# A transformer block with its backward pass on one core: w_o in 8 KB rows, P rebuilt between w_o tiles, gradient sections ahead of the last LayerNorm, w_down loads behind w_gate stores

**Chip, cores, metric.** One Trainium2 chip, one core. The metric is device time in microseconds (us), as a median over executions. In the views PE is the matmul engine, DVE the vector engine, ACT the scalar engine, POOL GpSimd and SP the sync engine. A load or store is split over sixteen DMA engines; what GpSimd issues (most stores, the w_up and w_gate loads) goes through queue 0, what the sync engine issues through queue 1.

## The reference

A decode step with adaptive LayerNorm, attention over the last 4096 positions of a key/value cache, and a gated feed-forward block (FFN), and then the gradients of all inputs:

```python
x = A_x                                            # 1 x 1 x 1024
mod = (silu(c) @ w_mod).reshape(1, 6, 1, -1)       # w_mod 1024 x 6144
sa, ca, ga, sb, cb, gb = (mod[:, i] for i in range(6))
h = layernorm(x) * (1 + ca) + sa
x = x + ga * attention(h, k_cache, v_cache, wq, wo)   # 32 heads of 128, 4 kv heads; wo 4096 x 1024
h = layernorm(x) * (1 + cb) + sb
x = x + gb * ((sigmoid(h @ w_gate) * (h @ w_up)) @ w_down)   # 1024 x 3584, 3584 x 1024
out, vjp = jax.vjp(...)                            # and the gradients of everything
# ... cut
```

Only one row of x exists. So a weight is read once (w_q and a part of w_mod a second time, for the gradients) and every weight gradient, an outer product of a column and a row, is written once. The cache gradients are full size (4 x 65536 x 128, twice) and zero outside the last 4096 positions; those zeros are 126 of the 256 MB moved. The kernel writes them in 120 stores of 1 MB and uses them as filler: lists of small integers (`Z_...`) say after which step how many go into GpSimd's DMA queue.

## The kernel before

One large on-chip arena is reused by stage. The parts that matter, with cuts:

```python
# forward: w_o, 2 KB rows
wo_view = A_wo.rearrange("(j p) n -> p j n", p=P)
def load_wo(q4):
    nc.sync.dma_start(out=wo_t[q4], in_=wo_view[:, q4 * 4:(q4 + 1) * 4, :])
# ... cut
# FFN loop, 14 blocks of 256 columns; w_down in 2 buffers, w_up and w_gate in 3
for n in range(NB):
    # ... dug, hh, broadcast of dug, FFN products
    nc.sync.dma_start(out=wd_dram(out_8, n), in_=wd)       # w_down gradient
    if n + 2 < NB:
        load_wd(n + 2)                                     # same buffer: waits for that store
    for j in range(KD):
        ttr(ug[:, :, j, :], ...)                           # DVE: dh2
        outer_act(ug[:, :, j, :], h2[:, j:j + 1], dug_b2)  # ACT: gradient in place
        # ... front(n + 1) at j == 3
    if n + 1 < NB:
        front_dve(n + 1)                                   # DVE: needs w_down of block n + 1
    nc.gpsimd.dma_start(out=dwu_view[...], in_=ug[:, 0, :, :])
    nc.gpsimd.dma_start(out=dwg_view[...], in_=ug[:, 1, :, :])
    zero(Z_FFN[2 * n])
    if n + 3 < NB:
        load_ug(n + 3)                                     # 512 B rows
    zero(Z_FFN[2 * n + 1])
# ... cut: broadcasts, P rebuilt; then dw_o tile by tile, w_q reloaded behind it
# last loop: w_q gradient, key/value gradients (two buffers), sections of the w_mod gradient
for i in range(KD):
    # ... dwq store
    grad_kv(gkv[8 * i:8 * i + 8], Z_DKV[i])                # PE, ACT copies to a buffer, store
    if i % 2 == 1:
        sec(2 + i // 2, Z_SEC[2 + i // 2])                 # DVE, store of 1 MB
# ... LayerNorm tail, dx and x2 through one row buffer, then:
sec(6, Z_SEC[6])
sec(7, Z_SEC[7])
for j in range(KD):
    # ... last eight stores, 512 KB each (ACT and DVE in turn)
    nc.gpsimd.dma_start(out=dwm_view[:, j, 0:2048], in_=s2_t[j])
```

## Time and profile before

| | before |
|---|---|
| time, three runs | 634.1 us (633.64 to 634.2) |
| profiled span | 632.7 us |
| bytes moved | 256.41 MB, 405 GB/s over the span |
| busy PE / DVE / ACT | 30% / 50% / 35% |

The DMA row and the table of stages are shown in the prediction. I read them with one more figure, the loss of a stage: its length less its bytes divided by 427 GB/s, the rate at which zeros alone are stored. It comes from the sizes and times of the trace's packets (the single transfers of the DMA engines). Before, in us: 3.6 in the first 8 us; 1.1 up to 100; 2.2 from there to the FFN; 14.3 in the FFN loop; 1.1 from there to 580; and 9.9 after 580.

### The profile page before, as it was taken

Reading aid. Unit: us, or ns where it says so; the run is one execution under the profiler, and the core shown is the slowest. Engines: PE = TensorE matmul, PEld = TensorE weight load, DVE = VectorE, ACT = ScalarE, POOL = GpSimd, SP = SyncE. Lnnn points to the kernel's source line nnn. Section 1 sums busy time; section 2 is a strip of 40 time slices with the busy share of each in tenths; the row PEclk is TensorE's granted clock in tenths of the full one; section 3 lists DMA queues with packets and bytes.
Section 4 is the critical chain, followed back from the end, with each engine's and each line's share of the span. In section 5 each row is a group of like instructions: output and inputs, shape, how many; then the busy total and the mean of one; then the engine's idle time right before and its main releaser. Section 6 shows DMA issues by size and latency. Waiting matters only on the chain.

```text
span 632.7 us, 8339 instructions
## 1 busy us (share of the span) xinstructions
PE 191.6 (30%) x3288; PEld 168.7 (27%) x3288; DVE 319.5 (50%) x708; ACT 222.5 (35%) x342; POOL 142.3 (22%) x224
## 2 busy tenths in 40 slices
PE   3865626650120211111111111115107800055600
PEld 3865624550120211111111111115105700044500
DVE  2532106500069383867527574467995800998060
ACT  1641215610000160613325333335696700055650
POOL 1100200220322213333135331432222211122120
PEclk9966659755555555555555555555555555555555
DMA  9999999999999999999999999999999999999976
GB/s 334 424 422 422 421 419 420 410 421 407 419 427 424 357 415 405 410 384 401 419 401 389 402 400 417 407 414 412 416 423 422 418 424 425 419 428 424 425 322 262
DMA packets 46279, 256.41 MB, mean 405 GB/s; under 512 B 4768, under 2 KB 4768, under 8 KB 23712
## 3 DMA queue, kind: packets, MB, share of 16 engines
q0 software_dynamic: 32128, 192.95, 79.8%
q1 hardware_dynamic: 14064, 62.93, 29.2%
q8 instruction: 25, 0.41, 0.2%
q14 instruction: 14, 0.11, 0.0%
q10 hardware_dynamic: 48, 0.01, 0.0%
HBM read 70.26 MB, written 185.60 MB: 404 GB/s over the span
## 4 chain that ended last, share of the span: by engine, by line
DMA 80%; issue 8%; PE 4%; POOL 3%; DVE 2%; ACT 1%; POOLq 0%; ACTq 0%; SPq 0%; DVEq 0%
DMA out_dram<-arena 28%; DMA out_dram<-zeros 24%; DMA arena<-in_A_wq_dram 9%; DMA arena<-in_A_v_cache_dram 6%; DMA arena<-in_B_w_gate_dram 5%; DMA arena<-in_A_wo_dram 4%; DMA arena<-in_B_w_down_dram 3%; PE tp_kv L401 1%; DMA rows<-in_c_dram 1%; POOL arena L488 1%; DVE junk L174 1%; PE bc_ps L585 1%; POOL out_dram L139 1%; ACT arena L404 0%; PE tp_pT L444 0%
## 5 line engine op out<-in xcount | busy, mean ns | idle before, releaser
L139 POOL DMA_DIRECT2D out_dram<-zeros x120 | 67.2, 565 | 222.6 <-DVE arena L166 43.7
L205 ACT ACTIVATE arena<-dug_b,h 128x512 bf16<-128x512 bf16 x112 | 71.4, 713 | 13.9 <-DVE dh2acc L174 13.9
L174 DVE CUSTOM_DVE_ANT_0 arena<-arena,dug_b 128x512 bf16<-128x512 bf16 x112 | 69.6, 684 | 0.3
L174 DVE CUSTOM_DVE_ANT_0 arena<-arena 128x1024 bf16<-128x1024 bf16 (+1 forms) x16 | 45.1, 2818 | 33.0 <-DMA arena<-in_w_mod_dram 30.7
L561 PE MATMUL gu_ps<-h_bf,arena 128*128 128x1 bf16 x448 | 15.7, 166 | 117.8 <-issue 86.9
L174 DVE CUSTOM_DVE_ANT_0 junk<-arena,b1k 128x1024 fp8e4<-128x1024 bf16 x28 | 34.2, 1223 | 26.4 <-DMA arena<-in_B_w_down_dram 25.9
L738 PEld LDWEIGHTS <-arena 8*128 8x128 bf16 x256 | 25.8, 131 | 76.1 <-issue 72.5
L561 PEld LDWEIGHTS <-arena 128*128 128x128 bf16 x448 | 14.0, 105 | 119.5 <-issue 87.3
L487 POOL DMA_DIRECT2D arena<-in_B_w_up_dram x14 | 12.9, 921 | 107.5 <-DMA out_dram<-arena 77.0
L174 DVE CUSTOM_DVE_ANT_0 arena<-arena,b1k 128x1024 bf16<-128x1024 bf16 x32 | 36.7, 1218 | 0.0
L742 ACT CAST arena<-ps_kv 128x512 bf16<-128x512 f32 x32 | 16.1, 692 | 50.8 <-DMA out_dram<-arena 50.8
L585 PE MATMUL bc_ps<-ident_bf,dug_bf 128*128 128x128 bf16 x56 | 14.5, 475 | 64.2 <-DVE hh L157 64.2
L563 ACT ACTIVATE sg<-gu_ps 128x2 f32<-128x2 f32 x14 | 2.3, 166 | 89.5 <-PE gu_ps L561 89.5
L205 ACT ACTIVATE arena<-b1k,o_col 128x1024 bf16<-128x1024 bf16 x32 | 33.4, 1148 | 0.0
L738 PE MATMUL ps_kv<-DO_hd,arena 8*128 8x128 bf16 x128 | 15.9, 295 | 50.8 <-ACT arena L742 50.8
L401 PE MATMUL tp_kv<-ident_bf,arena 128*128 128x128 bf16 x256 | 22.8, 257 | 22.8 <-DMA arena<-in_A_k_cache_dram 14.0
L313 PEld LDWEIGHTS <-arena 128*128 128x128 bf16 x320 | 28.7, 133 | 1.9 <-issue 1.9
L166 DVE COPY arena<-tp_kv 128x1024 bf16<-128x1024 bf16 x19 | 13.0, 691 | 30.8 <-PE tp_kv L401 30.8
L401 PEld LDWEIGHTS <-arena 128*128 128x128 bf16 x256 | 19.8, 118 | 25.8 <-DMA arena<-in_A_k_cache_dram 14.8
L157 DVE TENSOR_TENSOR dug<-dhh,sg 128x2 f32<-128x2 f32 x14 | 2.3, 161 | 47.2 <-ACT sg L563 46.7
L585 PEld LDWEIGHTS <-dug_bf 128*128 128x128 bf16 x56 | 7.8, 171 | 65.3 <-DVE hh L157 65.3
L404 ACT COPY arena<-tp_kv 128x1024 bf16<-128x1024 bf16 x13 | 13.2, 1012 | 33.9 <-PE tp_kv L401 33.9
(209 smaller groups left out, 504.2 us busy)
## 6 DMA issues: line engine op xcount, KB each, us to landing
out_dram<-zeros POOLq DMA_DIRECT2D x120, 1024.0 KB, 17.0
out_dram<-arena POOLq DMA_DIRECT2D x32, 1024.0 KB, 19.3
out_dram<-arena POOLq DMA_DIRECT2D x36, 512.0 KB, 12.1
arena<-in_A_wq_dram SPq DMA_DIRECT2D x16, 1024.0 KB, 12.4
arena<-in_w_mod_dram SPq DMA_DIRECT2D x8, 1536.0 KB, 18.5
arena<-in_A_wo_dram SPq DMA_DIRECT2D x8, 1024.0 KB, 43.5
arena<-in_B_w_down_dram SPq DMA_DIRECT2D x14, 512.0 KB, 9.3
arena<-in_B_w_up_dram POOLq DMA_DIRECT2D x14, 512.0 KB, 9.7
```

The lines of the kernel that those rows point to most:

```text
L139: ins = nc.gpsimd.dma_start(out=zleft.pop(0).bitcast(FP32), in_=zeros[:, :])
L166: return nc.vector.tensor_copy(out=out, in_=a)
L174: return nc.vector.tensor_tensor_reduce(out=out, in0=w, in1=b, scale=1.0, scalar=0.0, op0=ALU.mult, op1=ALU.add, accum_out=acc)
L205: return nc.scalar.activation(out=out, in_=b, func=ACT.Copy, scale=col)
L313: nc.tensor.transpose(tp[:, nb * P:(nb + 1) * P], wm_t[j][:, c0:c0 + P], ident_bf[:, :])
L401: nc.tensor.transpose(tp[:, t8 * P:(t8 + 1) * P], src[:, g, t_ * DH:(t_ + 1) * DH], ident_bf[:, :])
L404: last = nc.scalar.copy(out=o, in_=tp[:, :])
L487: nc.gpsimd.dma_start(out=ug_slot[n % 3][:, 0, :, :], in_=wu_view[:, :, n * FB:(n + 1) * FB])
L561: nc.tensor.matmul(gu[:, col + jj:col + jj + 1], lhsT=ug[:, k, j, jj::2], rhs=h2_bf[:, j:j + 1], start=(j == 0), stop=(j == KD - 1))
L585: nc.tensor.matmul(ps4[:, k // 2, :, k % 2], lhsT=r["dug_bf"][:, k:k + 1].broadcast_to([P, P]), rhs=ident_bf[:, :], start=(k == 0), stop=( ...
L738: nc.tensor.matmul(ps[:, t4 * DH:(t4 + 1) * DH], lhsT=rows[32 * g:32 * g + HG, t_ * P:(t_ + 1) * P], rhs=hd[32 * g:32 * g + HG, :], start= ...
L742: nc.scalar.copy(out=o, in_=ps[:, :])
```

## The change

Four intents, and new zero lists. w_o and its gradient move in 8 KB rows, which puts the head dimension in another order; o and do are brought into that order by small matmuls. P and the broadcasts are rebuilt between w_o tiles and not ahead of them. The last two gradient sections move into the last loop and x2 is written early, each with its own row buffer. The loads of w_down wait for the w_gate store of their block.

```diff
-Z_FFN = [2, 0, 2, 3, 2, 1, 2, 3, 3, 0, 2, 0, 3, 0, 2, 0, 2, 4, 2, 0, 3, 5, 0, 0, 1, 7, 0, 0]
+Z_FFN = [3, 0, 3, 1, 4, 0, 3, 1, 4, 0, 3, 0, 3, 0, 4, 2, 3, 2, 3, 1, 3, 6, 0, 3, 1, 7, 3, 1]
 ... the other lists too: 36 zero stores asked for ahead of the FFN loop (51 before), 64 in it (49 before)
-        rowb = pool.tile([8, P], BF16, name=name + "_orow", tag="orow")
+        rowb = pool.tile([8, P], BF16, name=name + "_orow", tag=name + "_orow")
+    def wo_rows(t, q4):
+        return t[q4 * 512:(q4 + 1) * 512, :].rearrange("(p j) n -> p (j n)", j=4)
-        nc.sync.dma_start(out=wo_t[q4], in_=wo_view[:, q4 * 4:(q4 + 1) * 4, :])
+        nc.sync.dma_start(out=wo_t[q4], in_=wo_rows(A_wo, q4))
 ... 16 small matmuls that shuffle o, and the like for do
-        if n + 2 < NB:
-            load_wd(n + 2)
 ...
-        nc.gpsimd.dma_start(out=dwg_view[:, :, n * FB:(n + 1) * FB], in_=ug[:, 1, :, :])
+        st = nc.gpsimd.dma_start(out=dwg_view[:, :, n * FB:(n + 1) * FB], in_=ug[:, 1, :, :])
+        if n + 2 < NB:
+            dep(load_wd(n + 2), st)
 ... x2 and its store, up to right after the FFN
-    bcast(dmod_bf[:, 16:48], 32, dmod_b4, "A")
 ... in the dw_o loop:
+            if jj == 3:
+                outer_dve(w, o_sh[:, h:h + 1], dattn_b)
+            else:
+                outer_act(w, o_sh[:, h:h + 1], dattn_b)
+        nc.gpsimd.dma_start(out=wo_rows(out_5, q4), in_=wo_t[q4])
+        if q4 < 2:
+            bcast(dmod_bf[:, 16 + 16 * q4:32 + 16 * q4], 16, dmod_b4[:, 2048 * q4:2048 * (q4 + 1)], "A")
+        elif q4 < 6:
+            rebuild_P(q4 - 2)
+        elif q4 == 6:
+            build_e()
 ... in the last loop:
-        if i % 2 == 1:
-            sec(2 + i // 2, Z_SEC[2 + i // 2])
+        if 1 <= i <= 6:
+            sec(1 + i, Z_SEC[1 + i])
 ...
-    sec(6, Z_SEC[6])
-    sec(7, Z_SEC[7])
```

More of the change, by code (lines that the diff above doesn't have):

```diff
@@ L39 @@
 Z_INIT = 1
-Z_MOD = [0, 1, 3, 0, 0, 2, 0, 0]
-Z_Q = [1, 0, 0, 0, 3, 0, 3, 0]
-Z_K = [1, 1, 0, 0]
-Z_V = [4, 0, 1, 1]
-Z_SM = 5
+Z_MOD = [1, 0, 0, 0, 0, 0, 0, 0]
+Z_Q = [0, 1, 0, 0, 0, 0, 4, 1]
+Z_K = [4, 0, 0, 1]
+Z_V = [1, 2, 0, 0]
+Z_SM = 3
 Z_O = 0
-Z_WO = [0, 0, 1, 0, 4, 0, 8, 1]
-Z_LN = 5
-Z_UG = [0, 0, 5]
-Z_FFN = [2, 0, 2, 3, 2, 1, 2, 3, 3, 0, 2, 0, 3, 0, 2, 0, 2, 4, 2, 0, 3, 5, 0, 0, 1, 7, 0, 0]
+Z_WO = [0, 0, 0, 0, 2, 0, 9, 0]
+Z_LN = 2
+Z_UG = [2, 0, 2]
+Z_FFN = [3, 0, 3, 1, 4, 0, 3, 1, 4, 0, 3, 0, 3, 0, 4, 2, 3, 2, 3, 1, 3, 6, 0, 3, 1, 7, 3, 1]
 Z_T0 = 1
-Z_DWO = [4, 3, 1, 0, 0, 0, 0, 1]
-Z_SEC = [1, 0, 1, 0, 1, 0, 4, 2]
-Z_DWQ = [3, 0, 1, 1, 0, 0, 0, 4]
-Z_DKV = [0, 0, 0, 0, 1, 4, 0, 5]
+Z_DWO = [3, 4, 0, 0, 1, 2, 0, 0]
+Z_SEC = [1, 1, 3, 0, 1, 1, 4, 1]
+Z_DWQ = [1, 0, 0, 1, 0, 0, 0, 6]
+Z_DKV = [0, 0, 4, 0, 3, 3, 1, 5]
 @with_exitstack
@@ L370 @@
     cp(q_col2[:, HQ:2 * HQ], q_ps[:, 0:HQ])
-    wo_view = A_wo.rearrange("(j p) n -> p j n", p=P)
+    def wo_rows(t, q4):
+        return t[q4 * 512:(q4 + 1) * 512, :].rearrange("(p j) n -> p (j n)", j=4)
     wo_off = [40, 48, 56, 32, 0, 8, 16, 24]
-    wo_t = [ar(A_OFF + o, 8).rearrange("p (j n) -> p j n", j=4) for o in wo_off]
+    wo_t = [ar(A_OFF + o, 8) for o in wo_off]
     def load_wo(q4):
-        nc.sync.dma_start(out=wo_t[q4], in_=wo_view[:, q4 * 4:(q4 + 1) * 4, :])
+        nc.sync.dma_start(out=wo_t[q4], in_=wo_rows(A_wo, q4))
     load_kv(A_v_cache, v_nat)
@@ L468 @@
     cp(o_col, o_ps[:, 0:HQ])
+    o_hl = hilo(o_col, HQ, "o_hl").rearrange("p (q a) k -> p q a k", a=4)
+    sh_ps = new_acc("sh_ps")
+    for a in range(4):
+        for jj in range(4):
+            nc.tensor.matmul(sh_ps[32 * a:32 * a + 32, jj * 16:(jj + 1) * 16], lhsT=ident_bf[:, jj::4],
+                             rhs=o_hl[:, :, a, :], start=True, stop=True, tile_position=(0, 32 * a))
+    o_sh = vt([P, HQ], "o_sh")
+    o_shv = o_sh.rearrange("p (q j) -> p j q", j=4)
+    sh_v = sh_ps.rearrange("p (j q k) -> p j q k", j=4, k=2)
+    cp(o_shv, sh_v[:, :, :, 1])
+    addv(o_shv, o_shv, sh_v[:, :, :, 0])
     o_bf = vt([P, HQ], "o_bf", BF16)
-    cp(o_bf, o_col)
+    cp(o_bf, o_sh)
     wg_view = B_w_gate.rearrange("(j p) n -> p j n", p=P)
@@ L483, in load_wd @@
     def load_wd(n):
-        nc.sync.dma_start(out=wd_slot[n % 2], in_=wd_dram(B_w_down, n))
+        return nc.sync.dma_start(out=wd_slot[n % 2], in_=wd_dram(B_w_down, n))
     def load_ug(n):
@@ L492 @@
         for k in range(KD):
-            mm = nc.tensor.matmul(attn_ps[:, k:k + 1], lhsT=wo_t[h // 4][:, h % 4, k * P:(k + 1) * P],
+            mm = nc.tensor.matmul(attn_ps[:, k:k + 1], lhsT=wo_t[h // 4][:, (h % 4) * D + k * P:(h % 4) * D + (k + 1) * P],
                                   rhs=o_bf[:, h:h + 1], start=(h == 0 and k == 0), stop=(h == HQ - 1),
@@ L631 @@
     zero(Z_T0)
+    x2 = vt([P, KD], "x2")
+    mulv(x2, gb, ffn)
+    addv(x2, x2, x1)
+    col_to_row_out(x2, out_0[0], "x2")
     dcs234 = matvec_T([w234_T[:, nb, :] for nb in range(KD)], hilo(dh2, KD, "dh2_hl"), "dcs234")
@@ L659, in sec, with rebuild_P @@
         zero(nz)
-    bcast(dmod_bf[:, 16:48], 32, dmod_b4, "A")
     sec_load(0)
     sec_load(1)
-    for tb in range(4):
+    def rebuild_P(tb):
         tp = new_tp("tp_P")
@@ L673, with build_e @@
         nc.scalar.copy(out=P_bf[:, tb * 1024:(tb + 1) * 1024], in_=tp[:, :])
-    do_col = vt([P, HQ], "do_col")
+    do_sh = vt([P, HQ], "do_sh")
+    e_sh = ar(F_OFF + 16, 1).rearrange("p (j d) -> p j d", j=4)
+    def build_e():
+        ps = new_ps("e_ps")
+        for jj in range(4):
+            for a in range(4):
+                nc.tensor.matmul(ps[32 * a:32 * a + 32, jj * P:(jj + 1) * P], lhsT=ident_bf[:, jj::4], rhs=ident_bf[:, :],
+                                 start=True, stop=True, tile_position=(0, 32 * a))
+        nc.scalar.copy(out=ar(F_OFF + 16, 1), in_=ps[:, :])
@@ L677 @@
     wq_t = [ar(A_OFF + o, 8) for o in wo_off]
-    dwo_view = out_5.rearrange("(j p) n -> p j n", p=P)
     for q4 in range(8):
-        for hh4 in range(4):
-            h = q4 * 4 + hh4
-            w = wo_t[q4][:, hh4, :]
-            ttr(w, w, dattn_b, do_col[:, h:h + 1])
-            outer_act(w, o_col[:, h:h + 1], dattn_b)
-        nc.gpsimd.dma_start(out=dwo_view[:, q4 * 4:(q4 + 1) * 4, :], in_=wo_t[q4])
-        zero(Z_DWO[q4])
+        for jj in range(4):
+            h = q4 * 4 + jj
+            w = wo_t[q4][:, jj * D:(jj + 1) * D]
+            ttr(w, w, dattn_b, do_sh[:, h:h + 1])
+            if jj == 3:
+                outer_dve(w, o_sh[:, h:h + 1], dattn_b)
+            else:
+                outer_act(w, o_sh[:, h:h + 1], dattn_b)
@@ L687 @@
+        nc.gpsimd.dma_start(out=wo_rows(out_5, q4), in_=wo_t[q4])
+        zero(Z_DWO[q4])
+        if q4 < 2:
[4 more added lines that the diff above has]
+            build_e()
         nc.sync.dma_start(out=wq_t[q4], in_=wq_view[:, q4, :])
     do_col2 = vt([P, 2 * HQ], "do_col2", BF16)
-    cp(do_col2[:, 0:HQ], do_col)
-    cp(do_col2[:, HQ:2 * HQ], do_col)
+    do_blk = ar(F_OFF + 17, 0.25)
@@ new lines @@
+    nc.vector.memset(do_blk, 0.0)
+    for a in range(4):
+        cp(do_blk[32 * a:32 * a + 32, a * HQ:(a + 1) * HQ], do_sh[32 * a:32 * a + 32, :])
+    do_bv = do_blk.rearrange("p (n j) -> p n j", j=4)
+    do_ps = new_acc("do_ps")
+    for jj in range(4):
+        nc.tensor.matmul(do_ps[:, 0:HQ], lhsT=e_sh[:, jj, :], rhs=do_bv[:, :, jj], start=(jj == 0), stop=(jj == 3))
+    do_v = do_ps[:, 0:HQ].rearrange("p (a q) -> p q a", a=4)
+    cp(do_col2[:, 0:HQ].rearrange("p (q a) -> p q a", a=4), do_v)
@@ L693 @@
+    cp(do_col2[:, HQ:2 * HQ].rearrange("p (q a) -> p q a", a=4), do_v)
     prod2 = vt([P, 2 * HQ], "prod2")
@@ L773 @@
     col_to_row_out(dx0, out_1[0], "dx0")
-    x2 = vt([P, KD], "x2")
-    mulv(x2, gb, ffn)
-    addv(x2, x2, x1)
-    col_to_row_out(x2, out_0[0], "x2")
-    sec(6, Z_SEC[6])
-    sec(7, Z_SEC[7])
     for j in range(KD):
```

## The prediction

> **What bounds the kernel now.** I read the page first: the busy shares, then the slices, then the DMA queues. No engine is near its limit (PE 30%, DVE 50%, ACT 35%), but the DMA row is full in all but the last two slices:
>
> ```profile
> DMA  9999999999999999999999999999999999999976
> GB/s 334 424 422 422 421 419 420 410 421 407 419 427 424 357 415 405 410 384 401 419 401 389 402 400 417 407 414 412 416 423 422 418 424 425 419 428 424 425 322 262
> DMA packets 46279, 256.41 MB, mean 405 GB/s; under 512 B 4768, under 2 KB 4768, under 8 KB 23712
> ...
> q0 software_dynamic: 32128, 192.95, 79.8%
> q1 hardware_dynamic: 14064, 62.93, 29.2%
> ```
>
> The two queues' shares add up to 109% of the span. So the time is bytes over rate: the change saves only if it moves bytes faster or fills a stretch in which the engines are idle. That has to be seen stage by stage; the windows view is next (columns after the window: busy of PE, weight loads, DVE, ACT, POOL with counts, granted clock, DMA share, GB/s):
>
> ```profile
> 64.00:72.00 8.00, 5.82 (x178) 5.74 (x176) 1.10 (x3) 2.84 (x3) 0.53 (x1) 0.71 1.03 423
> 152.00:164.00 12.00, 3.04 (x96) 2.79 (x96) 0.00 (x0) 0.00 (x0) 2.10 (x4) 0.50 1.07 404
> 176.00:192.00 16.00, 2.96 (x68) 2.82 (x69) 11.61 (x36) 0.20 (x1) 3.19 (x6) 0.50 1.15 427
> 212.00:220.00 8.00, 1.87 (x36) 1.71 (x37) 0.88 (x6) 0.23 (x2) 2.01 (x4) 0.50 1.04 309
> 224.00:440.00 216.00, 38.70 (x750) 35.73 (x750) 130.05 (x402) 81.80 (x157) 69.96 (x97) 0.50 1.12 405
> 440.00:604.00 164.00, 56.70 (x707) 44.79 (x704) 103.14 (x135) 80.01 (x121) 32.39 (x53) 0.51 1.11 423
> 604.00:612.00 8.00, 0.00 (x0) 0.00 (x0) 4.78 (x7) 5.25 (x3) 0.53 (x1) 0.50 0.59 245
> 612.00:628.00 16.00, 0.38 (x1) 0.08 (x1) 4.29 (x13) 0.00 (x0) 5.11 (x9) 0.50 0.96 375
> 628.00:632.70 4.70, 0.00 (x0) 0.00 (x0) 0.00 (x0) 0.00 (x0) 0.00 (x0) 0.50 0.01 3
> ```
>
> Zeros alone (8 KB rows, 176 to 192) go at 427 GB/s. w_q loads in 8 KB rows (64 to 72) reach 423, w_o loads in 2 KB rows (152 to 164) 404, and w_up and w_gate loads in 512 B rows (212 to 220) only 309, with a DMA share over 1: there the engines are busy, but slow. Only one stretch is idle: 604 to 612, share 0.59. At 427 the whole volume would take 256.41 MB / 427 = 600.5 us. The span is 32.2 us above that.
>
> To split the excess I counted the trace's packets in 4 us bins by queue and size and fitted one rate to each kind, as an estimate: zeros and other 8 KB stores 424; w_up and w_gate loads 328 (14.7 MB, 44.8 us, 10.4 over 427); their stores 384 (3.9 us over); w_o and w_mod loads in 2 KB rows 397; the 4 KB packets of dw_o and of the last stores 415. The first 8 us (249 GB/s) lose 3.3 us, the last 33 us about 10.
>
> The hole at 604 is explained by the timelines of POOL, which issues the stores, and of DVE:
>
> ```profile
> 598.74 0.53 POOL L658 DMA_DIRECT2D out_dram<-arena  x1
> 610.19 0.53 POOL L658 DMA_DIRECT2D out_dram<-arena  x1 [10.91 <-DVE arena L170]
> 612.65 0.53 POOL L658 DMA_DIRECT2D out_dram<-arena  x1 [1.93 <-DVE arena L170]
> 613.17 3.52 POOL L787 DMA_DIRECT2D out_dram<-arena  x6
> ```
>
> ```profile
> 602.87 0.17 DVE L157 TENSOR_TENSOR x<-x,x 128x8 f32<-128x8 f32 x1
> 607.15 0.28 DVE L166 CAST x_orow<-rp_x 8x128 bf16<-8x128 f32 x1 [4.11 <-DMA out_dram<-dx_orow]
> ```
>
> For 10.91 us POOL has nothing to issue. It waits for gradient section 6 of w_mod, and DVE makes that late: it first does the LayerNorm tail, then waits 4.11 us until dx_orow has left the one row buffer that x_orow shares. The last eight stores (L787) sit behind sections 6 and 7 in program order, though ACT had the first of them ready at about 603.4.
>
> **What the Trainium skill says.** "DMA: Bandwidth & Descriptors", § Specifications, gives a fabric ceiling of 435 GB/s for the 16 engines; the trace's best stage, 427, agrees, so no stage has hidden head room. § Why small descriptors are slow (HBM only), gives a fixed overhead for each packet, which weighs more the smaller the piece. The order 427, 404, 309 for 8 KB, 2 KB and 512 B rows agrees in direction. § Queues, rings and completion order (Arbitration) says that each engine round-robins between its queues packet by packet. The trace fits that: in 1 us bins in which queue 0 carried almost nothing but w_up and w_gate loads, the total was 303 GB/s with queue 1 empty, and 376 when queue 1 carried about 134 beside them.
>
> **The change part by part.**
>
> *w_o in 8 KB rows.* The 8.4 MB load goes from 397 to about 420 GB/s: 21.2 - 20.0 = 1.2 us. The dw_o store, also 8.4 MB, goes from 415 to 424: 20.2 - 19.8 = 0.4 us. The price is 16 small matmuls and five DVE instructions (0.07 to 0.3 us each) ahead of the w_o products, and as much again at the end of dw_o: 3 us of chain each time. Ahead of the w_o products it is hidden, since PE waits 27.4 us there for w_o to arrive; at the other end the transfers run on. Sum: -1.6 us.
>
> *P and the broadcasts between w_o tiles.* Before, ACT does eight broadcast copies (4.0 us) and four copies of P, and starts the first outer product at 450.88. DVE had the first reduction done at 438.8. So the first dw_o store comes some 12 us earlier. One outer product in four moves to DVE: 8 x 0.35 us more there (a 128x4096 one takes 1.29), 8 x 1.15 less on ACT. But from 440 to 604 the mean is 423 GB/s: queued zeros already fill that wait. What it frees is a few zeros for elsewhere. 0 us.
>
> *gb sections ahead of the last LayerNorm, x2 early, own row buffers.* This takes the 4.11 us wait, about 5 us of DVE work (two reductions of 1.2 and two products of 1.29) and the program order away from the last eight stores. Those then follow as soon as ACT has them, some 5 us after the last key/value gradient is issued, while 2 to 5 MB (5 to 12 us) should still be queued. Data from 604 to 628: 1.96 + 6.0 = 8.0 MB, of which 4.2 MB at 411 and 3.8 at 424 take 19.2 us in place of 24. A ragged end of about 0.9 us remains. Saved: 3.9 us. The 4.7 us after 628 stay.
>
> *w_down loads wait for w_gate stores, zeros dealt out anew.* Bytes are the same; 15 zeros move from ahead of the FFN loop into it (49 to 64). In the trace w_down loads are issued when the w_down store lands, 3 to 25 us before the w_gate store of that block does. They now start then, near the next w_up and w_gate loads. With all 7.3 MB beside such loads, these would run at an effective 350 instead of 328: 44.8 - 42.0 = 2.8 us. But three or four zeros lie in queue 0 between that store and the next load, so much of w_down will meet zeros instead. I take 0.8 us.
>
> Sum: 1.6 + 3.9 + 0.8 = 6.3 us; 634.1 - 6.3 = 627.8.
>
> **The rivals.**
>
> *The FFN loop becomes a chain.* The w_down buffers are two deep, so two blocks now take: w_down load 9.3 us to landing, 2.5 of reduction, 3.5 to the broadcast, 6.5 for the eight reductions and products, and 12.1 for the store to land, about 34 us. The transfers for two blocks are 2 x (3.15 MB + 4.6 zeros of 1.05) = 16 MB, 39 us at 410. So the added zeros cover the chain by 5 us. For the rival: stores took up to 19 us in places and zeros wait behind late stores in POOL's order. If it wins, the loop loses 3 to 10 us, and the total is 631 to 638.
>
> *The stretch ahead of the FFN starves, having 15 zeros fewer.* Against: loads plus remaining zeros there are 72 MB, 171 us, and I count 6 MB or more queued when the last w_o tiles can be asked for. If it happens, up to 4 us are lost: 632.
>
> *Pairing works fully and stores gain as well.* Then 3.5 us instead of 0.8, and the total is 625.
>
> *The hole only moves:* DVE now has 8.1 us of work in a step with a section, against 7.4 us of data (3 MB). But in the trace it had the sixth of these steps done at 578, 20 us before its data left. If it wins, the 3.9 us are lost again: 632.
>
> **How the range follows.** Only the tail is idle time, and rates are capped at 427, so to be over 2% faster (below 621.4) the FFN traffic would have to gain 7 us and the tail everything: 6%. Slower by over 2% needs a stalled FFN loop: 2%. I give 92% to within 2%. The range, 623 to 632, holds the sum with full pairing on one side and one rival coming true on the other.
>
> **What would show it.** Right: no slice below 0.9 of DMA until the last, POOL's 10.91 us wait gone, w_o alone near 420 GB/s, the FFN stretch longer in time (more zeros in it), its loads still near 330. Wrong: DMA shares under 1 inside the FFN loop or between 100 and 180 us, POOL waiting for ACT there, or w_up and w_gate loads near 380, which would make pairing the main gain.

## The result, and the profile after

The changed kernel took 633.34 us (633.23 to 633.42, four runs), the kernel before 634.15 beside it (633.64 to 635.55, four runs). The ratio is 0.9984, with an interval of 0.9966 to 1.0001. A ratio is the mean time of one kernel's fast runs over that of the other's fast runs of the same rounds, so it is not quite the ratio of the medians. "The same" was right; the predicted 627.8 us and its range of 623 to 632 were not.

The page of the changed kernel, its DMA row, its rate by slice and its packets:

```profile
DMA  9999999999999999999999999999999999999986
GB/s 358 422 420 421 420 420 418 425 425 426 420 377 404 400 409 406 400 406 391 395 405 419 400 400 407 421 416 427 415 424 425 423 423 427 420 427 423 398 332 246
DMA packets 42183, 256.42 MB, mean 406 GB/s; under 512 B 4768, under 2 KB 4768, under 8 KB 17568
```

The packets under 8 KB are fewer (23712 before), so the w_o part did its work. The last two slices still move only 332 and 246 GB/s (322 and 262 before). The losses by stage show no gain in the two stages where the prediction put most of its sum: the FFN loop loses what it lost, and the stretch after 580 us 1.3 us more.

| loss against 427 GB/s, us | 0-8 | 8-100 | 100 to FFN | FFN loop | to 580 | after 580 | span |
|---|---|---|---|---|---|---|---|
| before (FFN 208 to 462) | 3.6 | 1.1 | 2.2 | 14.3 | 1.1 | 9.9 | 632.7 |
| after (FFN 172 to 452) | 2.8 | 1.2 | 0.5 | 14.3 | 0.9 | 11.2 | 631.5 |

w_o alone ran at 420 GB/s (404 before), as predicted; a window of the changed kernel, columns as in the prediction:

```profile
128.00:136.00 8.00, 2.89 (x91) 2.64 (x90) 0.00 (x0) 0.00 (x0) 0.00 (x0) 0.50 1.01 420
```

In the FFN loop a wait has grown. First the waits of the kernel before (engine, tile and line, releaser; then total us, count, longest):

```profile
DVE junk L174 <- DMA arena<-in_B_w_down_dram: 25.9, 7, 9.4
...
POOL out_dram L605 <- ACT arena L205: 13.2, 3, 7.4
```

The same waits in the changed kernel, where the stores of w_up's gradient are at L618:

```profile
DVE junk L174 <- DMA arena<-in_B_w_down_dram: 110.8, 12, 20.3
POOL out_dram L618 <- ACT arena L205: 51.0, 9, 11.8
```

DVE now waits 111 us for w_down, and GpSimd 51 us for the gradients that come after it. The chain that ended last shows it too. In the kernel before:

```profile
DMA 80%; issue 8%; PE 4%; POOL 3%; DVE 2%; ACT 1%; POOLq 0%; ACTq 0%; SPq 0%; DVEq 0%
```

In the changed kernel:

```profile
DMA 64%; DVE 17%; PE 7%; issue 5%; ACT 3%; POOL 2%; ACTq 0%; SPq 0%; DVEq 0%; POOLq 0%
```

In the tail the 10.91 us wait for section 6 is gone, but GpSimd waits elsewhere, four times. Timeline of GpSimd in the changed kernel (start, duration, instruction; in brackets the wait before it), where L792 stores a key/value gradient and L826 the last eight; the rows left out store sections and w_q gradients:

```profile
592.41 0.53 POOL L792 DMA_DIRECT2D out_dram<-arena  x1 [10.73 <-ACT arena L790]
...
600.01 0.53 POOL L792 DMA_DIRECT2D out_dram<-arena  x1 [6.02 <-ACT arena L790]
...
607.56 0.53 POOL L792 DMA_DIRECT2D out_dram<-arena  x1 [5.97 <-ACT arena L790]
613.09 1.56 POOL L826 DMA_DIRECT2D out_dram<-arena  x2 [5.00 <-ACT arena L205]
```

And ACT, which makes those gradients, waits for one of its two buffers to have left:

```profile
588.09 4.03 ACT L790 ACTIVATE arena<-ps_kv 128x512 bf16<-128x512 f32 x8 [10.95 <-DMA out_dram<-arena]
```

The new lists also ask for 147 zero stores in all, and there are 120; the last is issued at 561 us (584 before). So I had two first theories: (A) the tail is held by the two key/value buffers and the missing filler, and (B) the w_down wait costs what the tail gained. Both had to be tried, since a wait on the page is not yet a loss.

### The profile page after: what moved, and what is told of

Same layout as the page of the kernel before. It is cut to its first block, busy times and chain, and to the rows that moved or that the text cites. A ratio compares the mean times of both kernels' runs of the same rounds, so it can differ in the third digit from the quotient of the medians.

```text
span 631.5 us, 8419 instructions
## 1 busy us (share of the span) xinstructions
PE 183.6 (29%) x3324; PEld 161.7 (26%) x3324; DVE 322.9 (51%) x726; ACT 215.4 (34%) x335; POOL 139.5 (22%) x224
## 4 chain that ended last, share of the span: by engine, by line
DMA 64%; DVE 17%; PE 7%; issue 5%; ACT 3%; POOL 2%; ACTq 0%; SPq 0%; DVEq 0%; POOLq 0%
DMA out_dram<-arena 25%; DMA arena<-in_B_w_down_dram 11%; DVE arena L174 7%; DMA arena<-in_A_wq_dram 7%; DMA arena<-in_A_v_cache_dram 6%; DMA arena<-in_B_w_gate_dram 5%; DMA arena<-in_A_wo_dram 4%; ACT arena L205 3%; DMA out_dram<-zeros 3%; DMA arena<-in_w_mod_dram 2%; DVE junk L174 2%; DVE arena L170 2%; DVE arena L178 1%; DVE fold_ps L178 1%; PE tp_kv L404 1%
## 5 line engine op out<-in xcount | busy, mean ns | idle before, releaser
L139 POOL DMA_DIRECT2D out_dram<-zeros x120 | 65.1, 547 | 209.1 <-DMA out_dram<-zeros 51.3
L174 DVE CUSTOM_DVE_ANT_0 junk<-arena,b1k 128x1024 fp8e4<-128x1024 bf16 x28 | 34.3, 1224 | 111.3 <-DMA arena<-in_B_w_down_dram 110.8
L602 ACT CAST dug_b<-bc_ps 128x512 bf16<-128x512 f32 x14 | 8.2, 586 | 159.4 <-PE bc_ps L600 159.4
L205 ACT ACTIVATE arena<-b1k,o_sh 128x1024 bf16<-128x1024 bf16 x24 | 27.2, 1152 | 11.0 <-DVE do_sh L174 11.0
L404 PE MATMUL tp_kv<-ident_bf,arena 128*128 128x128 bf16 x256 | 21.2, 246 | 23.7 <-DMA arena<-in_A_k_cache_dram 13.8
L790 ACT ACTIVATE arena<-ps_kv 128x512 bf16<-128x512 f32 x32 | 16.1, 625 | 29.0 <-DMA out_dram<-arena 29.0
L313 PEld LDWEIGHTS <-arena 128*128 128x128 bf16 x320 | 25.3, 122 | 0.0
L404 PEld LDWEIGHTS <-arena 128*128 128x128 bf16 x256 | 18.4, 112 | 26.5 <-DMA arena<-in_A_k_cache_dram 14.7
L618 POOL DMA_DIRECT2D out_dram<-arena x14 | 12.6, 902 | 56.1 <-ACT arena L205 51.0
L784 PE MATMUL ps_kv<-Q_hd,arena 8*128 8x128 bf16 x128 | 16.1, 295 | 29.1 <-ACT arena L790 29.1
## 6 DMA issues: line engine op xcount, KB each, us to landing
out_dram<-arena POOLq DMA_DIRECT2D x36, 512.0 KB, 11.5
arena<-in_B_w_up_dram POOLq DMA_DIRECT2D x14, 512.0 KB, 11.2
```

The lines of the kernel that those rows point to most:

```text
L139: ins = nc.gpsimd.dma_start(out=zleft.pop(0).bitcast(FP32), in_=zeros[:, :])
L174: return nc.vector.tensor_tensor_reduce(out=out, in0=w, in1=b, scale=1.0, scalar=0.0, op0=ALU.mult, op1=ALU.add, accum_out=acc)
L205: return nc.scalar.activation(out=out, in_=b, func=ACT.Copy, scale=col)
L313: nc.tensor.transpose(tp[:, nb * P:(nb + 1) * P], wm_t[j][:, c0:c0 + P], ident_bf[:, :])
L404: nc.tensor.transpose(tp[:, t8 * P:(t8 + 1) * P], src[:, g, t_ * DH:(t_ + 1) * DH], ident_bf[:, :])
L784: nc.tensor.matmul(ps[:, t4 * DH:(t4 + 1) * DH], lhsT=rows[32 * g:32 * g + HG, t_ * P:(t_ + 1) * P], rhs=hd[32 * g:32 * g + HG, :], start= ...
```

## The experiments

Each kernel ran beside the kernel before on the same chip; the groups of runs used three chips, so kernels are compared by ratio. "After" in an edit is the changed kernel. The expectations name runs by label: there e4 is experiment 5, e6r is 6, and e12 is 12. Ratios are against the kernel before, with their 95% intervals; in microseconds 0.001 is 0.63.

### 1. The w_o rows alone, with the shuffle matrix built early

Before, with the parts of the diff that touch w_o, o and do; `build_e` ahead of the dw_o loop.

```diff
+    ps = new_ps("e_ps")
+    ... 16 matmuls
+    nc.scalar.copy(out=ar(F_OFF + 16, 1), in_=ps[:, :])     # ahead of the loop over q4
```

> The kernel before with one part of the change alone: w_o read and dw_o written in 8 KB rows, o and do shuffled on TensorE, everything else as before. My theory: the rows gave what I predicted, 1.6 us, and the whole gain of the changed kernel is this part and a little of the start; expected 632.5 us against 634.1, ratio 0.9975, and from 152 to 164 us about 422 GB/s where there were 404. Rival: the shuffle's chain of instructions costs what the rows give, ratio 1.000.

Measured: 636.6 us, ratio 1.0038 (1.0025 to 1.0052). My own edit was flawed. The shuffle matrix lies in the buffer of the last w_up and w_gate block, so ACT's copy waited for their stores and the whole dw_o loop behind it. Windows of this kernel:

```profile
460.00:464.00 4.00, 0.00 (x0) 0.10 (x1) 4.00 (x9) 2.18 (x3) 0.00 (x0) 0.50 0.24 87
464.00:468.00 4.00, 0.00 (x0) 0.00 (x0) 4.00 (x9) 4.00 (x5) 1.14 (x3) 0.50 0.02 10
468.00:472.00 4.00, 0.00 (x0) 0.00 (x0) 4.00 (x8) 4.00 (x5) 2.51 (x5) 0.50 1.08 416
```

From the end of the FFN loop (461 us) to 580 us it loses 7.5 us, 6.7 more than the clean version of experiment 2, yet the time is only 3.7 us longer (ratio 1.0038 against 0.9979), because the tail lost 3 us less (6.8 against 9.8). That a hole costs less than its size was the first hint of the main finding.

### 2. The same with the matrix built behind the seventh tile, as in the changed kernel

> The first run again with its flaw mended: there the matrix for the back shuffle was built ahead of the dw_o loop, in a place where the last w_up and w_gate store was still reading, so ACT waited and the DMA queues ran dry from 460 to 468 us. Here it is built at the seventh w_o tile, as in the changed kernel. Expected for 8 KB rows alone: 632.8 us, ratio 0.998 (1.3 us, what the first run gained ahead of the FFN loop). Rival: no gain, ratio 1.000, because the rate over all 16 DMA engines is not what sets the end.

One reduction writes its unused product in fp8. Built again with that product in bf16, in a tile that also holds the row buffers:

```diff
-    junk = vt([P, D], "junk", FP8)
+    junk = vt([P, D], "junk", BF16)      # early; rows24 and the row buffers are slices of it
```

> The first run again with its flaw mended: there the matrix for the back shuffle was built ahead of the dw_o loop, in a place where the last w_up and w_gate store was still reading, so ACT waited and the DMA queues ran dry from 460 to 468 us. Here it is built at the seventh w_o tile, as in the changed kernel. (The scratch output of the reductions over w_down is bf16 here, since its fp8 form was refused; no engine but DVE sees it.) Expected for 8 KB rows alone: 632.8 us, ratio 0.998 (1.3 us, what the first run gained ahead of the FFN loop). Rival: no gain, ratio 1.000, because the rate over all 16 DMA engines is not what sets the end.

Measured: 632.7 us, ratio 0.9979 (0.9967 to 0.9992): -1.3 us. The prediction's -1.6 us for the rows lies within the interval.

### 3. The tail part alone

Before, with sections in steps 1 to 6, x2 early and own row buffers:

```diff
-        if i % 2 == 1:
-            sec(2 + i // 2, Z_SEC[2 + i // 2])
+        if 1 <= i <= 6:
+            sec(1 + i, Z_SEC[1 + i])
```

> The kernel before with the tail part alone: sections 2 to 7 of w_mod in steps 1 to 6, x2 early, one row buffer for each output row. The step that I predicted at -3.9 us. Theory A (store order): the last key/value stores wait for their two buffers, the stores behind them on POOL wait too, and no zeros are left to fill, so the idle time only moves; expected within 1 us of before (633 to 635). Rival B (the prediction's step holds, and something else in the changed kernel took it back): 630.2, ratio 0.994.

Measured: 633.71 us, ratio 0.9994 (0.9981 to 1.0006). The predicted -3.9 us is not there, though the hole is nearly closed: from 608 to 612 us the kernel before moved 125 GB/s, this one 375. The idle time has gone to the end. Windows of this kernel:

```profile
608.00:612.00 4.00, 0.37 (x1) 0.08 (x1) 2.81 (x7) 3.97 (x4) 1.55 (x2) 0.50 0.90 375
624.00:628.00 4.00, 0.00 (x0) 0.00 (x0) 0.00 (x0) 0.00 (x0) 0.00 (x0) 0.50 0.06 26
```

The stage after 580 us loses 9.7 us, against 9.9 before. Theory A's time came, and the idle time did move, but to the end, where, as experiment 5 shows, one engine is still writing.

### 4. After without the w_down wait

```diff
+        if n + 2 < NB:
+            load_wd(n + 2)                  # right behind the w_down store, as before
-        if n + 2 < NB:
-            dep(load_wd(n + 2), st)
```

> The changed kernel with w_down loads issued as before, right after the w_down store, without the added wait. Theory C: queue 0 and 1 are full in the FFN loop in either case and 512 B rows set its rate, so nothing changes: 633.3 +- 0.7, and the loss against 427 GB/s inside the loop stays at 14 us. Rival D: the wait makes DVE sit idle 111 us for w_down and costs the loop what pairing gives; without it 2 to 3 us faster or slower.

Measured: 630.78 us, ratio 0.9946 (0.9933 to 0.9958): 2.4 us faster than the changed kernel (0.9984 - 0.9946), and beyond both intervals. The FFN loop loses 12.1 us in place of 14.3. DVE's wait for w_down falls from 110.8 to 30.3 us:

```profile
DVE junk L174 <- DMA arena<-in_B_w_down_dram: 30.3, 8, 7.0
```

Rival D holds and theory C fails: the wait does harm. It is not what the tail gained, as (B) had it, since experiment 3 shows a gain of 0.4 us there.

### 5. After with four key/value buffers

```diff
-            dst = ar(C_OFF + 8 * (g % 2), 8)
+            dst = ar((C_OFF, C_OFF + 8, G_OFF, G_OFF + 8)[g], 8)
```

> The changed kernel with four buffers for the key/value gradients in place of two (the two added ones are free after sections 0 and 1 have been stored). It takes away what makes the late key/value copies wait. Theory A (store order behind two buffers): the waits of 10.95 us of ACT for a store go, POOL is not held up, the dips from 588 to 614 us close, and the time falls by 3 to 5 us: 628.3 to 630.3. Rival E (DVE is late with the sections, 8.1 us of work in a step): nothing changes, 633.3. Rival F (the end is ragged because the 16 DMA engines finish apart): under 1 us.

Measured: 632.86 us, ratio 0.9978 (0.9965 to 0.9990), against 0.9984 for the changed kernel: no difference that the intervals would show. The holes did close. Windows of this kernel:

```profile
600.00:616.00 16.00, 0.00 (x0) 0.00 (x0) 1.61 (x3) 4.04 (x3) 3.19 (x6) 0.50 1.00 419
622.00:624.00 2.00, 0.00 (x0) 0.00 (x0) 0.00 (x0) 0.00 (x0) 0.00 (x0) 0.50 0.15 58
624.00:626.00 2.00, 0.00 (x0) 0.00 (x0) 0.00 (x0) 0.00 (x0) 0.00 (x0) 0.50 0.06 25
626.00:628.00 2.00, 0.00 (x0) 0.00 (x0) 0.00 (x0) 0.00 (x0) 0.00 (x0) 0.50 0.06 25
```

The first of the last eight stores is issued at 601.62, 11.5 us earlier than after's 613.09. From 600 to 616 the rate is 419 GB/s. But what was saved comes back at the end: from 624 to 628 the share is 0.06 and the rate 25 GB/s. One engine in sixteen is a share of 0.0625, and one sixteenth of 427 is 27 GB/s. So a single DMA engine is still writing. Theory A fell; rival F of the expectation (under 1 us, a ragged end) came true, and its sharper form is the third theory (G): **one of the sixteen engines is behind the others, and it alone sets the end.**

The same signature was in the kernel before. These windows are its "hole", in steps of 1 us:

```profile
608.00:609.00 1.00, 0.00 (x0) 0.00 (x0) 0.96 (x3) 0.00 (x0) 0.00 (x0) 0.50 0.23 92
609.00:610.00 1.00, 0.00 (x0) 0.00 (x0) 1.00 (x2) 0.72 (x1) 0.00 (x0) 0.50 0.08 33
610.00:611.00 1.00, 0.00 (x0) 0.00 (x0) 1.00 (x2) 1.00 (x1) 0.53 (x1) 0.50 0.09 33
611.00:612.00 1.00, 0.00 (x0) 0.00 (x0) 0.96 (x3) 0.28 (x1) 0.00 (x0) 0.50 0.82 344
```

A share of 0.08 is not zero: it is one engine and a little. The hole was idle time of fifteen engines only.

The trace says it a second way. Each store raises its semaphore sixteen times. The Trainium skill, "DMA: Bandwidth & Descriptors", § Why a DMA increments its semaphore by 16 and not by 1, says that these are the completions of single engines; so the times of the sixteen rises are sixteen landings. The landings of one store of the kernel before (issued at 598.74), one of experiment 5 (issued at 599.16) and one of experiment 12 below (issued at 602.76), sorted, in us:

```
before         606.8 607.0 607.1 607.2 607.7 607.9 608.0 608.1 608.1 608.3 608.5 608.9 608.9 609.1 609.6 | 614.2
experiment 5   608.6 608.7 609.0 609.8 609.9 610.3 610.4 610.4 610.8 610.9 611.1 611.2 611.6 611.8 612.0 | 618.4
experiment 12  608.8 608.8 608.9 608.9 608.9 608.9 608.9 608.9 608.9 608.9 608.9 608.9 608.9 609.0 609.0 | 609.0
```

In the first two, fifteen engines land within 3.4 us and the sixteenth 4.6 and 6.4 us behind them. Before's store was finished by the sixteenth at 614.2, after GpSimd had given the next one out at 610.19: that engine never ran dry in the hole. Nor was it slow there. The last landings of the next two stores of 1 MB came at 616.6 and 619.1, one each 2.4 to 2.5 us, and a sixteenth of 1 MB at a sixteenth of 427 GB/s takes 2.45 us. It was only behind.

A rival is that late issues set the end. In experiment 5 the last two stores are issued only at 618.25 and 618.92, since ACT waited 5.41 us to 615.96 for their buffer. But what it waited for was the store issued at 596.66, whose last share landed at 615.88. So this wait, too, is one for the last engine.

### 6. After without the w_down wait, with four key/value buffers

```diff
+        if n + 2 < NB:
+            load_wd(n + 2)                  # as in experiment 4
-            dst = ar(C_OFF + 8 * (g % 2), 8)
+            dst = ar((C_OFF, C_OFF + 8, G_OFF, G_OFF + 8)[g], 8)
```

> The changed kernel without the w_down wait and with four key/value buffers. Theory G: the end is set by one straggling DMA engine, which in the run with four buffers landed its share of every late store 6.3 us after the fifteenth and was busy to the end while the others idled; filling the idle time of the others gives nothing. Expected 630.5 us, within 0.5 of the run without the w_down wait (630.8). Theory A (idle time in the tail is what counts): with both, 3 to 4 us less, 627.

Built again as said under experiment 2:

> The changed kernel without the w_down wait and with four key/value buffers (scratch output bf16). Theory G: the end is set by one straggling DMA engine, which in the run with four buffers landed its share of every late store 6.3 us after the fifteenth and was busy to the end while the others idled; filling the idle time of the others gives nothing. Expected 630.5 us, within 0.5 of the run without the w_down wait (630.8). Theory A (idle time in the tail is what counts): with both, 3 to 4 us less, 627.

Measured: 630.59 us, ratio 0.9946 (0.9933 to 0.9958), the same as experiment 4. The landings of the very last store, in us from the start of the span, put experiments 3 to 6 side by side:

| kernel | 8th engine | 15th engine | last engine | span |
|---|---|---|---|---|
| before | 627.4 | 628.3 | 629.1 | 632.7 |
| 3: before, tail part | 623.3 | 624.4 | 628.3 | 631.9 |
| after | 625.8 | 626.6 | 628.5 | 631.5 |
| 5: after, four buffers | 622.5 | 623.3 | 628.3 | 631.2 |
| 4: after, no w_down wait | 623.4 | 624.2 | 626.1 | 629.0 |
| 6: the same, four buffers | 620.3 | 621.2 | 626.1 | 629.0 |

In each of the three pairs the middle engine is done 3.1 to 4.1 us earlier once the holes are closed, as the prediction had worked out from the mean rate (3.9 us), and the last engine 0.8, 0.2 and 0.0 us earlier. Theory G made the forecast for experiment 6 and it held.

### 7. Less work for some engine: zero stores of 120 partitions

If the laggard were the engine that a store of 120 partitions leaves out, such stores would let it catch up. The same page and section of the Trainium skill says that some copies of GpSimd's queue give ceil(partitions/16) partitions to each engine, so that 120 partitions would reach fifteen.

```diff
+            for n in ([120] * 4 + [P] * 11 + [32] if last else [P] * 15):
+                zregions.append(region[r0 * ZW:(r0 + n) * ZW].rearrange("(p x) -> p x", p=n))
```

> The changed kernel without the w_down wait, in which four late zero stores use 120 partitions in place of 128 (the bytes left over go in one store of 32 partitions; results are the same). If a store of 120 partitions leaves the last of the 16 DMA engines out, that engine has 4 x 65.5 KB = 0.26 MB less to move, 9.8 us at 26.7 GB/s, and each other engine 0.017 MB more, 0.65 us. Theory G with the straggler being that engine: its lag goes from about 6 us to below 1, and the time falls by 4 to 6 us, to 625 to 627. If the straggler is another engine: 0 to 1 us slower, 631 to 632, the lag as before. Theory A: no change.

Refused, and built again:

> The changed kernel without the w_down wait, in which four late zero stores use 120 partitions in place of 128 (the bytes left over go in one store of 32 partitions; results are the same; scratch output bf16). If a store of 120 partitions leaves the last of the 16 DMA engines out, that engine has 4 x 65.5 KB = 0.26 MB less to move, 9.8 us at 26.7 GB/s, and each other engine 0.017 MB more, 0.65 us. Theory G with the straggler being that engine: its lag goes from about 6 us to below 1, and the time falls by 4 to 6 us, to 625 to 627. If the straggler is another engine: 0 to 1 us slower, 631 to 632, the lag as before. Theory A: no change.

Measured: 631.28 us, ratio 0.9959 (0.9946 to 0.9971). One engine did get ahead by some 9 us in the landings, so fifteen engines share such a store, as the page has it. But in the last loop the last engine still trailed the fifteenth by 5 to 6 us, and the time is the 631 to 632 us forecast for that case. The laggard is another engine than the one left out.

### 8. After without the w_down wait, late loads on the queue of the stores

The lag of the last engine, read from the landings along the run of experiment 4, grows in the FFN loop and jumps between 500 and 540 us (last behind fifteenth: 5.3 us at 497, 11.5 at 511), while the w_q and section loads run on the second queue. So I put these on GpSimd's queue:

```diff
-        nc.sync.dma_start(out=wq_t[q4], in_=wq_view[:, q4, :])
+        if q4 >= 2:
+            nc.gpsimd.dma_start(out=wq_t[q4 - 2], in_=wq_view[:, q4 - 2, :])
 ... and the last two behind the loop; the section loads likewise
```

> The changed kernel without its w_down wait, with the late w_q and section loads issued by GpSimd onto the queue of the stores, so that no second queue runs after the last w_down store. If two queues side by side make one engine fall behind, the jump of its lag at 500 to 540 us is gone, the last engine lands within 3 us of the fifteenth at the end (6 before), and the time is 626.5 to 628.5 us (ratio 0.988 to 0.991). If the lag has another cause, the last engine still trails by 5 to 6 us and the time is 630 to 632.5 (ratio 0.9935 to 0.9975), the upper end if GpSimd's waits for buffers hold the stores up. I give the first 0.4.

Measured: 634.25 us, ratio 1.0003 (0.9991 to 1.0016). The jump is gone (6.0 us from 510 to 522), which fits the second queue as its maker; the edit also moved the loads in time and left gaps in the queue, so this is not shown. The 6 us were there without it, and GpSimd waited for buffers, up to 8.99 us at a time, with its queue running dry. Windows of this kernel:

```profile
510.00:526.00 16.00, 0.00 (x0) 0.00 (x0) 0.00 (x0) 0.00 (x0) 3.50 (x7) 0.50 0.75 296
```

The forecast of 626.5 to 628.5 us failed, and the time is above the other theory's 630 to 632.5 as well. I had taken the danger of GpSimd's waits too lightly. At the end the last engine trails by 2.6 us, but the gaps had let it catch up, so this run does not tell what the jump costs.

### 9. After without the w_down wait, with the zero lists of the kernel before

Rows (-1.3), tail (-0.4) and wait (+2.4) add up to +0.7 us, but the changed kernel is 1.0 us faster. Two more parts were left, which the prediction had put at nearly nothing.

```diff
-Z_FFN = [3, 0, 3, 1, 4, 0, 3, 1, 4, 0, 3, 0, 3, 0, 4, 2, 3, 2, 3, 1, 3, 6, 0, 3, 1, 7, 3, 1]
+Z_FFN = [2, 0, 2, 3, 2, 1, 2, 3, 3, 0, 2, 0, 3, 0, 2, 0, 2, 4, 2, 0, 3, 5, 0, 0, 1, 7, 0, 0]
 ... and all other lists
```

> The changed kernel without its w_down wait (630.8 us, ratio 0.9946 before) with the zero lists of the kernel before. The prediction put the new lists at -0.3 us. If the lists hold what the measured parts leave over (some -1.7 us), this runs at 632 to 632.7, ratio 0.997 or more; if the place of the zeros does not matter while each queue has work, it stays within 0.5 us of 630.8 (ratio 0.994 to 0.9955). I lean to the second with 0.55, since filling idle time of the other fifteen engines gained nothing in e4 and e6r.

Measured: 632.74 us, ratio 0.9979 (0.9966 to 0.9993). Against experiment 4 that is +2.1 us: the new lists are worth 2 us, against my leaning. The FFN loop loses 14.8 us with the old lists and 12.1 with the new.

### 10. The same as experiment 4, with P and the broadcasts ahead of the w_o loop

```diff
+    bcast(dmod_bf[:, 16:48], 32, dmod_b4, "A")
+    for tb in range(4):
+        rebuild_P(tb)
 ... and the calls between the tiles taken out
```

> The changed kernel without its w_down wait, but with the broadcasts of the modulation gradient and all four parts of P ahead of the w_o loop, as before. The prediction put this move at 0. If it holds what is left over, 632 to 632.7 us (ratio 0.997 or more), and the first w_o store comes some 5 us later with a dip in the rate near 455 to 465 us; if not, 630.5 to 631.3 (ratio 0.994 to 0.9955).

Measured: 630.86 us, ratio 0.9950 (0.9936 to 0.9964), against 0.9946. The place of P is worth nothing that shows, as predicted. The edit took effect: ACT's first outer product of dw_o comes at 432.61 us, against 419.92 in experiment 4. But the first w_o store is issued at 449.5 in both, and not 5 us later as I had expected, because five zero stores stand ahead of it and GpSimd waits about 2 us before each for an earlier store to land. The run also carries the bf16 scratch tile, so that change costs nothing either.

### 11. What the 512 B rows cost (wrong results on purpose)

After, with the w_up and w_gate loads read as contiguous 4 KB rows of the same bytes. The numbers computed from them are wrong.

```diff
+            flat = t.rearrange("a b -> (a b)")[n * P * KD * FB:(n + 1) * P * KD * FB]
+            nc.gpsimd.dma_start(out=ug_slot[n % 3][:, k, :, :].rearrange("p j f -> p (j f)"),
+                                in_=flat.rearrange("(p x) -> p x", p=P))
```

> The changed kernel with w_up and w_gate read in contiguous 4 KB rows, which gives wrong results on purpose: it measures what their 512 B rows cost. My fit gave 10.4 us over the 427 GB/s rate for these loads. If that is right and lies on the path: 623 to 625 us, and the loss in the FFN loop falls from 14 to about 4 us. Rival: the loads' slowness is hidden behind the two block chain of w_down, and less than 3 us come off.

Refused, and built again:

> The changed kernel with w_up and w_gate read in contiguous 4 KB rows, which gives wrong results on purpose: it measures what their 512 B rows cost (scratch output bf16). My fit gave 10.4 us over the 427 GB/s rate for these loads. If that is right and lies on the path: 623 to 625 us, and the loss in the FFN loop falls from 14 to about 4 us. Rival: the loads' slowness is hidden behind the two block chain of w_down, and less than 3 us come off.

Measured: 627.22 us, ratio 0.9894 (0.9878 to 0.9909): 5.7 us under the changed kernel. The FFN loop loses 7.8 us in place of 14.3. The forecast (4 us there, 623 to 625 in all) went too far, and so did the rival (under 3 us). The short rows are still the largest single cost that an experiment here isolates.

### 12. and 13. Nine and nineteen more zero stores in the FFN loop

Experiment 4, with zero stores moved into the loop from behind it. If filler beside the short loads were the reason for experiment 9, more of it should help more.

```diff
-Z_FFN = [3, 0, 3, 1, 4, 0, 3, 1, 4, 0, 3, 0, 3, 0, 4, 2, 3, 2, 3, 1, 3, 6, 0, 3, 1, 7, 3, 1]
+Z_FFN = [3, 1, 3, 2, 4, 1, 3, 2, 4, 1, 3, 1, 3, 1, 4, 2, 3, 2, 3, 2, 3, 6, 0, 3, 1, 7, 3, 2]
 ... in 13: nineteen more, and the lists behind the loop all 0
```

> The changed kernel without its w_down wait, with nine more zero stores inside the FFN loop, taken from the last loop (they would have been written from 480 to 560 us). If the loop's loss falls with each zero store in it as it did between the two lists (2.7 us for 15), its loss goes from 12.1 to 10.5 us and the time to 629.2 to 630 us if the last loop keeps the rate without them; if the loop is filled already, its loss stays within 0.5 us of 12.1 and the time is 630.5 to 631.5.

> As e12, with nineteen more, so that no zero store is left after the FFN loop. If the loss falls with each, the loop loses 8.7 us in place of 12.1; but the w_o stage and the stage to 580 us have no filler then, and I expect 2 to 5 us lost there in place of 0.7: 629.5 to 632.5 us. If the loop is filled already, 632.5 to 636 us.

Measured: 635.2 us, ratio 1.0016 (1.0003 to 1.0028), and 638.05 us, ratio 1.0061 (1.0047 to 1.0074). The loop loses 13.0 and 12.9 us, no less than 12.1, so it was filled already. Both times lie above the worse forecast, since the stretch behind the loop ran short. Windows of experiment 12:

```profile
566.00:584.00 18.00, 10.03 (x81) 7.99 (x80) 17.86 (x13) 9.42 (x19) 3.19 (x6) 0.50 0.82 335
```

These two are the counter-test of theory G. Here the holes are longer than the lag: the laggard catches up (last landing 0.1 and 0.4 us behind the fifteenth at the end, against 1.9 in experiment 4), all sixteen engines run dry together, and then the holes do cost time. In experiment 12 the span grew by 4.2 us.

## Why the prediction was wrong, point by point

**The class of the result was right, the size was wrong:** within 2% was given 92%, but -6.3 us were summed up and -1.0 came (0.0016 of 634).

**w_o in 8 KB rows, -1.6: right.** -1.3 measured alone, and 404 became 420 GB/s.

**P and the broadcasts, 0: right.** Experiment 10 differs by 0.0004. A step on the way was wrong: the first dw_o store did not come 12 us earlier (451.8 us, 455.4 before), and in experiments 4 and 10 the place of P has no part in when it comes.

**Sections ahead of the last LayerNorm, -3.9: the step that failed.** The prediction took the hole as time in which "the engines" were idle and divided bytes by the mean rate. The mean over sixteen engines hides that one of them was at work all through it. The holes that are closed (experiments 3, 5 and 6) bring the middle engine forward by 3.1 to 4.1 us and the last one by 0.8, 0.2 and 0.0. The prediction allowed "a ragged end of about 0.9 us"; the ragged end is 3.9 us in experiment 3 and 5.0 in experiment 5. Closing the hole frees the fifteen, and the sixteenth, which sets the end, has as much left to write as before. The prediction's rival "the hole only moves" did come about in the changed kernel, through the key/value buffers and the exhausted zeros and not through DVE, but experiment 5 shows that this did not matter.

**w_down wait and zeros, -0.8: +0.3 measured, near by luck, since two wrong terms cancel.** The wait costs 2.4 us (experiment 4), the lists gain 2.1 (experiment 9). In the FFN loop they cancel: 14.3 us lost before and after. The prediction named the harm as a rival ("becomes a chain") but judged that the zeros cover the chain, and it looked for the wrong sign, DMA shares under 1. In windows of 4 us the share stays at 1 but for one window of 0.97; DVE's waits grew, and the loop lost 2.2 us more than without the wait. The next w_down load now starts 2 to 22 us after the w_down store has landed (at most 2.6 before), when the w_gate store lands. (In the kernel before, the w_gate store landed 2.7 to 37.5 us after that load was issued, not the 3 to 25 that the prediction read.) The rival's 3 to 10 us for the loop were nearer than the prediction's gain.

Why the loop lost that is not shown by an experiment. I read the packets in bins of 1 us; which of them are w_up and w_gate loads is worked out from the order of issue, so the numbers are estimates. The pairing that the wait was meant to bring about came: beside nearly pure w_up and w_gate loads (over 80% of the bytes of their queue) the second queue moved about 6 MB, against 3.3 before. But next to experiment 4 the wait also gathered more of these loads in such bins, about 7 MB against 5, away from the long stores. Such bins lose about 0.6 us for each MB of loads with the wait and 0.5 to 0.6 without it; bins in which the loads are only 20 to 50% lose about 0.4 (experiment 4). So the company of w_down shows no gain next to experiment 4. With the old zero lists (before, and experiment 9) about 9 MB lie in the nearly pure bins, at about 0.7 us each, which fits what the new lists gain.

**The sum by measured parts:** -1.3 - 0.4 + 2.4 - 2.1 = -1.4 us, against -1.0 measured. Each term has an interval of some 0.8 us either way, so nothing is missing that could be seen.

**What stays open.** Which engine lags, and why. The landings carry no number, and that it is the same engine each time is inferred from the lag persisting from store to store. In experiment 4 the lag grows from 0.1 us at 200 us to 3.5 at 450, in the FFN loop. The Trainium skill, "DMA: Bandwidth & Descriptors", § Latency and other measured facts, says that engines 7 and 15 are usually slower than the others, with a guess at the reason. A single engine that falls behind agrees with that in kind, though in the tail it moved at a full sixteenth of the rate. By that page's order of engines experiment 7 would rule out engine 15; no run here shows whether it is engine 7. Why the old zero lists cost 2.7 us more in the loop is open as well: experiments 12 and 13 rule out the mere number of zeros there from 64 up, not what they stand beside.

**The best version** is experiment 4, equal to 6 within their intervals: the changed kernel without the w_down wait, 630.78 us. It beats the kernel before by 0.54% (0.9946) and the changed kernel by 0.4%.

## What to carry to other kernels

When DMA is the bound, ask how many engines are busy in a hole before pricing it: a share of 0.06 to 0.09 is one engine out of sixteen, and the end belongs to the last engine, so in these runs a hole cost little as long as it was shorter than that engine's lag. Read the sixteen landings of a late store before working on the tail. And judge a new wait inside a loop by what its engines wait for and by the rate, not by the DMA share alone, which stayed full here while 2.4 us were lost.

## What the Trainium skill lacked or had wrong

- "DMA: Bandwidth & Descriptors", § Latency and other measured facts, tells of slower engines, but not how far one falls behind over a long run. Here the last landing of a late store trails the fifteenth by 4.6 us before and by 6.4 us in experiment 5, and closing holes of up to 4 us in the other fifteen's work gained under 1 us.
- The same page, § Where 436 GB/s comes from, says that the HBM side (about 358 GB/s) binds transfers between HBM and on-chip memory. That sentence does not hold for one core alone: here the whole run averages 406 GB/s of such transfers and stages of zero stores reach 427. The fabric ceiling of 435, not 358, was the useful bound. The page's own single-core measurement (425 for 16 MB) says the same.
- No page gives a measured rate of loads in short rows for this chip, alone or beside other traffic. Here w_up and w_gate loads in 512 B rows ran at 309 GB/s with little beside them, and reading the same bytes in 4 KB rows brought the loss of that loop from 14.3 to 7.8 us.
